# Loading the identity once per head for the scores, and moving a layer's last wo rows in sixteen transfers of eight rows

## The chip, the cores and the metric

The kernel runs on one core of one Trainium2 chip. The metric is the device time of one execution in microseconds (us), lower is better. A profiled run gives a trace; the *span* that its page states is about 2 us shorter than the measured time of the same run. Runs of a one-core program are called fast or slow by how they stand to the fastest run of the same kernel.

## The reference

Four attention layers for one token, in the order A, B, A, B. Each has 32 heads, a cache of 8,192 positions and a head width of 192; the model width is 640. Everything is bfloat16.

```python
def layer(x, k_cache, v_cache, wq, wo):              # cut: names, the key and value repeat (factor 1)
    q = (layernorm(x) @ wq).reshape(B, Sq, 32, 192).transpose(0, 2, 1, 3)
    scores = einsum("bhqd,bhkd->bhqk", q, k_cache) * 192 ** -0.5
    o = einsum("bhqk,bhkd->bhqd", softmax(scores), v_cache)
    return o.transpose(0, 2, 1, 3).reshape(B, Sq, 32 * 192) @ wo
x = x + layer(x, *A); x = x + layer(x, *B); x = x + layer(x, *A); x = x + layer(x, *B)
```

K and V of one head are 3 MB each, and nearly all of them are read in every layer that uses them. So the kernel reads 849 MB and does little arithmetic on each byte.

## The kernel before

All large transfers are issued by one sequencer, SP, into eight buffers `slot[0..7]` of 128 partitions x 24,576 bytes. A K or V tile fills one buffer, one packet of 24,576 bytes for each partition (32,000 such packets in the trace, for 250 tiles). In the trace each transfer adds 16 increments to its semaphore (4,544 for 284 transfers), within 8.6 us for one V tile at the turn of layers; I take each for the landing of the share of one of the 16 DMA engines that the page counts. A reader waits for all 16. SP issues a transfer as soon as the buffer's last reader is done.

The wo matrix of a layer comes in three transfers of 10 heads each and a small last one, "wol", with the rows of the last two heads. It goes into unused columns of the third one's buffer:

```python
if n[0] == "wol":
    wol = slot[place[("wo", l, 2)]][:, NW * D:(NW + OI) * D].rearrange("p (i n) -> p i n", n=D)
    return SP.op(lambda s: s.dma_start(
        wol, w["wo"][o["wol"] * DH:(o["wol"] + O_LAST) * DH].rearrange("(p i) n -> p i n", p=P)),
        sem=semOL, inc=16)
```

OI is 3, so this is 128 partitions x 3 x 640 elements of 2 bytes, 3,840 bytes for each partition.

The scores of a head: DVE multiplies K by q in four chunks; PE then adds up the products over the head width, with the identity as stationary matrix, in 24 matmuls of 512 columns:

```python
for c in range(4):
    PE.wait(chunks[c])
    for r in range(QD // R):
        d0 = c * QD + r * R
        fin = c == 3 and r == QD // R - 1
        e = PE.op(lambda t, d0=d0, fin=fin: t.matmul(S[:, :], lhsT=ident[:], rhs=k3[:, :, d0:d0 + R],
                                                     start=(d0 == 0), stop=fin), signal=fin, bank=use[f"S{par}"])
```

Each of these matmuls is two instructions: a weight load (PEld) of `ident` and the matmul proper (3,072 of each on the page below).

## Time and profile before

| what | value |
|---|---|
| time | 2005.2 us, median of 3 runs (2005.04 to 2006.86) |
| bytes read | 849.35 MB, 424 GB/s over the span |
| main DMA queue (q1) | busy 99.2% of 16 engines' span |
| PE program refills (q8) | 82 packets, 1.34 MB |
| PE busy, DVE busy | 70%, 52% |

These are lines of the page of the kernel before. The first line of part 1 gives busy time, share of the span and number of instructions of each engine; GB/s is by 40 equal slices of the span; then come two DMA queues (packets, MB, share of 16 engines) and two groups of instructions (busy us, mean ns of one, idle time before them).

```profile
PE 1402.4 (70%) x10438; PEld 616.8 (31%) x10438; DVE 1047.3 (52%) x1072; ACT 217.2 (11%) x657; POOL 4.6 (0%) x22
...
GB/s 404 431 430 430 429 430 426 430 431 429 425 431 429 431 429 430 426 431 430 429 361 431 430 430 430 431 426 429 429 430 426 430 428 428 431 430 431 430 430 325
...
q1 hardware_dynamic: 43824, 849.37, 99.2%
q8 instruction: 82, 1.34, 0.3%
...
L437 PE MATMUL S<-slot,ident 128*128 128x512 bf16 x3072 | 839.5, 429 | 286.6 <-DVE slot L425 286.6
L437 PEld LDWEIGHTS S<-slot,ident 128*128 128x128 bf16 x3072 | 307.8, 108 | 813.2 <-DVE slot L425 428.3
```

What to see: the DMA engines have no spare time, at 430 GB/s in nearly every slice. Only the first slice, the one at the turn from layer 1 to layer 2 (361) and the last fall clearly short. The 3,072 weight loads overlap PE's matmuls. So only what DMA engines do can change the time much.

SP's timeline at the end of layer 1 (start, us, line; x2 means two issues):

```profile
1004.11 0.33 SPq L269 DMA_DIRECT2D slot<-in_B_wo_dram  x1
1004.48 0.43 SPq L252 DMA_DIRECT2D slot<-in_B_wo_dram  x1
1009.29 15.91 SPq L264 DMA_DIRECT2D slot<-in_A_wq_dram  x2
```

And the end of the chain of waits (start, us, what):

```profile
1996.69 1.44 PE TB L503 x12
1998.13 3.71 PE YB L394 x90
2001.86 0.16 DVE x_bf L548
```

The last work is PE's output projection (YB).

One more reading, of the 16 increments of a semaphore, is not printed by any view, but the trace has it. The 16 shares of the first K tile land within 1.1 us. Those of a V tile issued at 987.51 land over 8.6 us (1006.65 to 1015.26), and those of the last K tile over 8.2 us (1967.86 to 1976.03). Refills do this: each packet of 16,384 bytes takes about 1.0 to 1.1 us on one engine, and that engine then stays about 1.55 us behind.

### The profile page before, as it was taken

How to read it: one execution, taken by the hardware profiler on the slowest of the kernel's cores; microseconds unless marked ns; L12 is line 12 of the kernel's file. 1: busy time of each engine (PE TensorE's matmuls, PEld its weight loads, DVE VectorE, ACT ScalarE, POOL GpSimd, SP SyncE). 2: the span in 40 equal slices, each digit the busy share in tenths (PEclk: the TensorE clock that was granted, in tenths of full speed). 3: DMA queues.
4: the chain of work that ended last, by engine and by line, in shares of the span. 5: the costliest groups of instructions: out<-in, count | busy, mean ns of one | idle time of the engine just before them, and what ended most of it. 6: DMA issues, size and time to landing. Idle time of an engine off the chain costs nothing.

```text
span 2005.0 us, 23356 instructions
## 1 busy us (share of the span) xinstructions
PE 1402.4 (70%) x10438; PEld 616.8 (31%) x10438; DVE 1047.3 (52%) x1072; ACT 217.2 (11%) x657; POOL 4.6 (0%) x22
## 2 busy tenths in 40 slices
PE   5677767767666767667777676676777767767667
PEld 2223223223332322322342232232234323323223
DVE  3454554556345456455536545545654455654554
ACT  0011011011011111111100111111110111111110
POOL 0000000000000000000000000000000000000000
PEclk9788888788678788878778888888886888987887
DMA  9999999999999999999989999999999999999997
GB/s 404 431 430 430 429 430 426 430 431 429 425 431 429 431 429 430 426 431 430 429 361 431 430 430 430 431 426 429 429 430 426 430 428 428 431 430 431 430 430 325
DMA packets 44067, 850.85 MB, mean 424 GB/s; under 512 B 4800, under 2 KB 7360, under 8 KB 7872
## 3 DMA queue, kind: packets, MB, share of 16 engines
q1 hardware_dynamic: 43824, 849.37, 99.2%
q8 instruction: 82, 1.34, 0.3%
q14 instruction: 17, 0.14, 0.0%
q10 hardware_dynamic: 144, 0.00, 0.0%
HBM read 849.35 MB, written 0.00 MB: 424 GB/s over the span
## 4 chain that ended last, share of the span: by engine, by line
DMA 67%; PE 19%; DVE 12%; ACT 1%; issue 1%; another core or an unknown queue 0%; POOL 0%; DVEq 0%; ACTq 0%
DMA slot<-in_A_k_cache_dram 33%; DMA slot<-in_B_k_cache_dram 32%; PE S L437 13%; DVE slot L425 10%; PE O L473 2%; DMA slot<-in_A_wq_dram 1%; PE TB L488 1%; DVE s_sb L444 1%; DMA x_bf<-in_A_x_dram 1%; ACT p_sb L454 1%; PE QT L358 1%; PE YB L394 1%; PE TB L458 0%; DVE small L451 0%
## 5 line engine op out<-in xcount | busy, mean ns | idle before, releaser
L425 DVE TENSOR_TENSOR slot<-slot,q_sb 128x3072 bf16<-128x3072 bf16 x512 | 865.9, 1754 | 461.2 <-DMA slot<-in_A_k_cache_dram 236.2
L437 PE MATMUL S<-slot,ident 128*128 128x512 bf16 x3072 | 839.5, 429 | 286.6 <-DVE slot L425 286.6
L437 PEld LDWEIGHTS S<-slot,ident 128*128 128x128 bf16 x3072 | 307.8, 108 | 813.2 <-DVE slot L425 428.3
L473 PE MATMUL O<-slot,p_sb 128*2 128x384 bf16 x4096 | 347.0, 420 | 0.0
L444 DVE TENSOR_REDUCE s_sb<-S 128x64 f32<-128x512 f32 x128 | 88.4, 691 | 248.6 <-PE S L437 248.6
L473 PEld LDWEIGHTS O<-slot,p_sb 128*2 128x2 bf16 x4096 | 128.5, 88 | 133.4 <-issue 97.6
L488 PE MATMUL TB<-o_sb,small 128*1 128x192 f32 x480 | 121.5, 385 | 36.6 <-DVE small L462 28.2
L384 ACT ACTIVATE q_sb<-QM 128x192 bf16<-128x192 f32 x120 | 39.6, 330 | 982.4 <-PE QM L377 982.4
L458 PE MATMUL TB<-small,ones 128*128 128x1 f32 x256 | 50.1, 265 | 110.0 <-ACT p_sb L454 110.0
L448 PE MATMUL QM<-ident,m_bf 128*128 128x128 bf16 x128 | 27.8, 217 | 129.6 <-DVE m_bf L447 129.6
L481 ACT ACTIVATE o_sb<-O,small 128x384 f32<-128x384 f32 x128 | 74.3, 580 | 231.0 <-PE O L473 231.0
L462 DVE RECIPROCAL small<-TB 128x1 f32<-128x1 f32 x128 | 21.6, 169 | 122.7 <-PE TB L458 122.7
L458 PEld LDWEIGHTS TB<-small,ones 128*128 128x128 f32 x256 | 39.3, 193 | 129.7 <-ACT p_sb L454 129.7
L454 ACT ACTIVATE p_sb<-s_sb,small 128x64 bf16<-128x64 f32 x128 | 44.5, 348 | 290.1 <-DVE small L451 290.1
L451 DVE TENSOR_REDUCE small<-QM 128x1 f32<-128x128 f32 x128 | 37.3, 292 | 53.7 <-PE QM L448 53.7
L494 ACT ACTIVATE orow<-TB 1x192 bf16<-1x192 f32 x120 | 38.3, 319 | 202.6 <-PE TB L488 202.6
L488 PEld LDWEIGHTS TB<-o_sb,small 128*1 128x1 f32 x480 | 33.2, 88 | 78.4 <-DVE small L462 37.4
L448 PEld LDWEIGHTS QM<-ident,m_bf 128*128 128x128 bf16 x128 | 12.3, 96 | 146.5 <-ACT q_sb L384 131.6
L394 PE MATMUL YB<-oT,slot 128*128 128x1 bf16 x900 | 37.9, 178 | 3.4 <-ACT oT L409 2.2
L394 PEld LDWEIGHTS YB<-oT,slot 128*128 128x128 bf16 x900 | 36.9, 131 | 4.2 <-ACT oT L409 2.9
L377 PEld LDWEIGHTS QM<-ident,qT 128*128 128x128 bf16 x240 | 23.0, 99 | 30.5 <-issue 1.9
L377 PE MATMUL QM<-ident,qT 128*128 128x128 bf16 x240 | 30.4, 209 | 1.6 <-ACT qT L366 1.6
(46 smaller groups left out, 191.0 us busy)
## 6 DMA issues: line engine op xcount, KB each, us to landing
slot<-in_B_k_cache_dram SPq DMA_DIRECT2D x64, 3072.0 KB, 36.1
slot<-in_A_k_cache_dram SPq DMA_DIRECT2D x63, 3072.0 KB, 23.4
slot<-in_A_v_cache_dram SPq DMA_DIRECT2D x63, 3072.0 KB, 25.9
slot<-in_B_v_cache_dram SPq DMA_DIRECT2D x60, 3072.0 KB, 37.5
slot<-in_A_wo_dram SPq DMA_DIRECT2D x6, 2400.0 KB, 26.7
slot<-in_B_wo_dram SPq DMA_DIRECT2D x6, 2400.0 KB, 34.9
slot<-in_A_wq_dram SPq DMA_DIRECT2D x4, 2880.0 KB, 22.5
slot<-in_B_wq_dram SPq DMA_DIRECT2D x4, 2880.0 KB, 29.7
```

What stands on the lines that cost most here:

```text
L377: e = PE.op(lambda t, b=b, o=o, n=n, d=done: t.matmul(QM[:, d:d + n], lhsT=qT[:, b:b + 1].broadcast_to([P, P]), rhs=ident[:, o:o + n], sta ...
L384: lambda a: a.activation(q_sb[i][:], QM[:, 0:DH], ACT.Copy), e, last["q"][i], bank=use["QM"])
L394: e = PE.op(lambda t, i=i, c=c, f=y_first[0], fin=fin: t.matmul(YB[:, c:c + 1], lhsT=t3[:, i, c:D:DC], rhs=o[:, i:i + 1], start=f, stop=fi ...
L425: e = DV.op(lambda v, d0=d0: v.tensor_tensor(k3[:, :, d0:d0 + QD], kin[:, :, d0:d0 + QD], q_sb[qi][:, d0:d0 + QD].unsqueeze(1).broadcast_t ...
L437: e = PE.op(lambda t, d0=d0, fin=fin: t.matmul(S[:, :], lhsT=ident[:], rhs=k3[:, :, d0:d0 + R], start=(d0 == 0), stop=fin), signal=fin, ba ...
L444: ev_s = DV.op(lambda v: v.tensor_reduce(s_sb[par][:], S[:].rearrange("p (j r) -> p j r", r=R), AX.X, ALU.add), ev_S[h], last["s"][par], b ...
L448: e = PE.op(lambda t: t.matmul(QM[:, C_MX:C_MX + P], lhsT=m_bf[par][:, 0:1].broadcast_to([P, P]), rhs=ident[:], start=True, stop=True), ev ...
L454: ev_p[h] = AC.op(lambda a: a.activation(p_sb[par][:], s_sb[par][:], ACT.Exp, bias=negm[par][:, 0:1], accum_out=l_col[par][:]), ev_n, ev_s ...
L458: e = PE.op(lambda t: t.matmul(TB[:, C_L + par:C_L + par + 1], lhsT=ones[:], rhs=l_col[par][:], start=True, stop=True), ev_p[h], last["L"] ...
L473: e = PE.op(lambda e, g=g, j=j, f=m < G, fin=fin: e.matmul(OB[par][32 * g:32 * g + 2, 0:2 * DH], lhsT=p_sb[par][:, j:j + 2], rhs=t[:, j * ...
L481: lambda a: a.activation(o_sb[:], OB[par][:, 0:2 * DH], ACT.Copy, scale=rl[par][:, 0:1]),
L488: e = PE.op(lambda t, i=i: t.matmul(TB[0:1, C_O:C_O + DH], lhsT=pick[:, i:i + 1], rhs=o_sb[:, i * DH:(i + 1) * DH], start=(i == 0), stop=( ...
```

## The change

The intent is, first, to load the identity once per head and let 23 of 24 score matmuls use what the PE array already holds. Second, wol's one transfer becomes 16 transfers of 8 rows each. Each is meant to be served by only 8 engines, so that the idle front-runners may take load from the others.

```diff
+def matmul_held(t, out, lhsT, rhs, start, stop):
+    return t.add_instruction(mybir.InstMatmult(
+        ...                      # cut: name, engine, operands, tile size and position
+        start_tensor_calc=start, stop_tensor_calc=stop, ldweights=False))
@@ wol
-                return SP.op(lambda s: s.dma_start(
-                    wol, w["wo"][o["wol"] * DH:(o["wol"] + O_LAST) * DH].rearrange("(p i) n -> p i n", p=P)),
-                    sem=semOL, inc=16)
+                src = w["wo"][o["wol"] * DH:(o["wol"] + O_LAST) * DH].rearrange("(p i) n -> p i n", p=P)
+                for r in (r + b for r in range(0, P, 32) for b in range(4)):
+                    e = SP.op(lambda s, r=r: s.dma_start(wol[r:r + 29:4], src[r:r + 29:4]), sem=semOL, inc=16)
+                return e
@@ scores
-                        e = PE.op(lambda t, d0=d0, fin=fin: t.matmul(S[:, :], lhsT=ident[:], rhs=k3[:, :, d0:d0 + R],
-                                                                     start=(d0 == 0), stop=fin), signal=fin, bank=use[f"S{par}"])
+                        e = PE.op(lambda t, d0=d0, fin=fin: (
+                            t.matmul(S[:, :], lhsT=ident[:], rhs=k3[:, :, d0:d0 + R], start=True, stop=fin) if d0 == 0 else
+                            matmul_held(t, S[:, :], ident[:], k3[:, :, d0:d0 + R], False, fin)), signal=fin, bank=use[f"S{par}"])
```

More of the change, by code (lines that the diff above doesn't have):

```diff
@@ L53, in emit @@
                     ins.then_inc(it[1], it[2])
+def matmul_held(t, out, lhsT, rhs, start, stop):
+    return t.add_instruction(mybir.InstMatmult(
+        name=t.bass.get_next_instruction_name(), engine=mybir.EngineType.PE,
+        ins=[t.lower_ap(rhs), t.lower_ap(lhsT, for_matmul_weights=True)], outs=[t.lower_ap(out)],
+        start_tensor_calc=start, stop_tensor_calc=stop, tile_size=(128, 128), tile_position=(0, 0), ldweights=False))
 HEADS_W = 10
```

## The prediction

> **What bounds the kernel now.** Transfers: the page shows 849 MB on the main queue, 99.2% of 16 engines' time, 430 GB/s in nearly every slice; only the first slice, the one at the turn from layer 1 to 2 (361) and the last (325) fall clearly short. In the chain of waits DMA has 67%, and DVE waits 2 to 3 us for each K tile. So what counts is when the *last* of the 16 engines delivers its share. The trace's semaphore landings show how unequal they are: the 16 increments of the first K tile arrive within 1.1 us, those of the last V tiles of layer 1 within 8.6 us (1006.7 to 1015.3), within 1.6 us after the turn of layers, within 8.2 us at the end (K head 31: 1967.9 to 1976.0). About eight engines lag 6 to 8.6 us, about six not at all.
>
> The lag comes from the second queue, "instruction": 82 packets of 16,384 bytes, 1.0 to 1.1 us each, about every 24 us. 82 x 16,384 bytes over PE's 20,876 instructions is 64 bytes each, so this is PE's program being refilled[...]. Where one falls, one engine's landing moves back by 1.54 to 1.56 us for good, until queues run dry at the turn.
>
> **What the change does.**
> 1. Held identity: 128 heads x 23 = 2,944 weight loads fewer. On PE they are hidden: six warm 512-column matmuls take 1.47 us, about 216 ns apart, and in a cold stretch about 427 ns apart, weight loads beside them. PE gains next to nothing. But 2,944 x 64 bytes is 11.5 refills less: 11.5 x 1.55 us over about eight lagging engines is 2.2 us (estimate).
> 2. The wo rows: 16 issues of about 0.33 us instead of one of 0.43 us, 4.9 us more on a sequencer that mostly waits for buffers. At the turn 1 to 2 they start at 1004.5 and the next issue is at 1009.3, so at most about 0.5 us slips. Eight rows should give a transfer eight engines[...]. A row of 3,840 bytes takes 149 ns, so eight engines lose 8 x 0.149 = 1.2 us a layer and eight gain as much. [...]
>
> **Critical path.** What lagging engines save reaches the end: the last K tile lands earlier and the 29 us after it stay. Gain 2.2 us plus 0 to 3.6 us; I put 3 in 4 on the favourable engines. So near 2001 us, 0.2% faster.
>
> **What would show it.** Refills near 70; weight loads 7,494; matmul spacing unchanged; spread of landings about 5 us at the turn and 6 to 7 us at the end instead of 8.6 and 8.2; wo rows of layer 3 landed before the previous transfer's slowest share.
>
> **What would make it wrong.** Eight rows served by lagging engines (then about 2006 us); small transfers that cost far more than their bytes; a lower PE clock with fewer PE instructions, which lengthens the tail by 1 to 2 us; a queue sequencer held up at the turn of layers.

The forecast's sum was 2.2 us from the refills plus 0 to 3.6 us from the rows (three layers of 1.2 us), and with 3 in 4 on the second term near 2001 us. The second term needs the engines that serve eight rows to be those that lead. That was the assumption, which no trace of the kernel before shows. Eight engines for eight rows was an assumption as well.

## More of the kernel before

The next view counts busy time in stretches around the end of layer 0, where the wo rows of that layer land. After the stretch and its length come busy us and instructions of PE, PEld, DVE, ACT, POOL; then the granted PE clock, the DMA engines' busy share and GB/s.

```profile
490.00:505.00 15.00, 12.00 (x55) 5.34 (x57) 11.28 (x14) 0.88 (x4) 0.00 (x0) 0.93 1.01 430
505.00:520.00 15.00, 12.49 (x184) 8.94 (x177) 1.36 (x11) 1.50 (x4) 0.55 (x1) 0.53 1.01 428
520.00:535.00 15.00, 10.28 (x62) 3.87 (x59) 8.14 (x8) 1.17 (x4) 0.00 (x0) 0.73 1.01 426
```

The one 128-row transfer of the wo rows (507 to 514 us) leaves no dent: 428 GB/s.

## The result, and the profile after

| | median us | range | runs |
|---|---|---|---|
| before, same rounds | 2006.03 | 2005.04 to 2007.02 | 4 |
| after | 2014.1 | 2011.47 to 2014.65 | 4 |

The ratio is 1.0038, with a 95% interval of 1.002 to 1.0055. Ratios here and below are the mean time of one kernel's fast runs over that of the other's of the same rounds, so they are not quite the ratio of the medians that are quoted. The kernel is 0.4% slower, where 0.2% faster was predicted.

The same parts of the page of the kernel after:

```profile
PE 1404.1 (70%) x10438; PEld 321.1 (16%) x7494; DVE 1047.2 (52%) x1072; ACT 217.6 (11%) x657; POOL 4.7 (0%) x22
...
GB/s 404 431 431 429 431 430 425 429 431 431 397 431 430 430 429 430 426 431 430 430 338 429 429 430 429 432 428 429 429 430 398 431 428 431 430 428 430 430 431 331
...
q8 instruction: 70, 1.15, 0.2%
...
L58 PE MATMUL S<-slot,ident 128*128 128x512 bf16 x2944 | 802.6, 427 | 33.7 <-DVE slot L434 33.6
...
L447 PEld LDWEIGHTS S<-slot,ident 128*128 128x128 bf16 x128 | 12.7, 99 | 337.0 <-DVE slot L434 329.7
```

The weight loads fell to 7,494 and the refills to 70, as meant, and a matmul takes what it took. The loss stands in the GB/s row: three slices fell, slice 11 (425 to 397), slice 21 (361 to 338) and slice 31 (426 to 398). These are the ends of layers 0, 1 and 2. The others are within 3 of what they were, but for the last (325 to 331).

The stretches at the end of layer 0, after:

```profile
490.00:505.00 15.00, 11.79 (x79) 1.54 (x39) 9.76 (x13) 1.00 (x5) 0.00 (x0) 0.96 1.00 430
505.00:520.00 15.00, 9.91 (x149) 7.85 (x150) 0.95 (x9) 1.38 (x4) 0.00 (x0) 0.50 1.02 339
520.00:535.00 15.00, 9.97 (x29) 0.63 (x6) 7.93 (x8) 0.73 (x2) 0.55 (x1) 0.61 0.99 420
```

In the stretch with the wo rows the engines are busy all the time (share 1.02), but they move 339 GB/s instead of 428. That is 15 x (428 - 339) / 428 = 3.1 us of transfers lost. They did not wait; packets took longer, as their records below show.

SP's timeline at the end of layer 1, and the end of the chain, both after:

```profile
1006.15 0.33 SPq L278 DMA_DIRECT2D slot<-in_B_wo_dram  x1
1006.52 10.65 SPq L262 DMA_DIRECT2D slot<-in_B_wo_dram  x16
1017.22 12.36 SPq L273 DMA_DIRECT2D slot<-in_A_wq_dram  x2
```

```profile
1972.12 36.39 DMA slot<-in_B_wo_dram
2008.51 0.14 issue
2008.64 0.75 PE YB L403 x15
2009.41 0.16 DVE x_bf L558
```

The 16 issues take 10.65 us (623 ns for one), where I had put 4.9 us, and the next issue starts 7.9 us later than before. At the end, the last 15 matmuls wait for the last wo rows, which landed at 2008.51. Both look like suspects. Experiments show that the first is none.

The packet records of the trace say which packets got longer. Around the landing of wol in layer 0:

| packets of | before, mean ns | after, mean ns | extra engine time, us (over 149, 717 and 914 ns) |
|---|---|---|---|
| 3,840 B (the wo rows) | 151 | 224 | 9.6 |
| 19,200 B (the wo transfer ahead) | 718 | 893 | 11.3 |
| 24,576 B (K and V around it) | 933 | 1,505 | 29.5 |

Together that is 50.4 us of engine time, or 3.2 us for each of 16 engines in the mean. The same sum is 37.9 us at the end of layer 1 (there mostly packets of wq, 11,520 bytes) and 52.6 us at that of layer 2, so 2.4 and 3.3 us. The three make 8.8 us. The landings of the first tile behind wol agree: the mean of its 16 increments is later than before by 2.83 us after layer 0, 5.48 us after layer 1, 8.56 us after layer 2 (the last increment by 2.45, 5.69 and 8.46 us); the program ends 7.6 us later in these traces. So longer packets account for the loss, and the rows themselves make up less than a fifth of what they cost in layer 0.

### The profile page after: what moved, and what is told of

Its sections match the earlier page's. It is cut to its first block, busy times and chain, and to the rows that moved or that the text cites. A ratio compares the mean times of both kernels' runs of the same rounds, so it can differ in the third digit from the quotient of the medians.

```text
span 2012.6 us, 20472 instructions
## 1 busy us (share of the span) xinstructions
PE 1404.1 (70%) x10438; PEld 321.1 (16%) x7494; DVE 1047.2 (52%) x1072; ACT 217.6 (11%) x657; POOL 4.7 (0%) x22
## 4 chain that ended last, share of the span: by engine, by line
DMA 68%; PE 17%; DVE 12%; SPq 2%; ACT 1%; issue 1%; another core or an unknown queue 1%; POOL 0%; DVEq 0%; ACTq 0%
DMA slot<-in_A_k_cache_dram 33%; DMA slot<-in_B_k_cache_dram 31%; PE S L58 12%; DVE slot L434 10%; DMA slot<-in_B_wo_dram 2%; SPq L262 2%; PE O L483 2%; DMA slot<-in_A_wq_dram 1%; PE S L447 1%; PE TB L498 1%; DVE s_sb L454 1%; DMA x_bf<-in_A_x_dram 1%; ACT p_sb L464 0%; PE TB L468 0%
## 5 line engine op out<-in xcount | busy, mean ns | idle before, releaser
L58 PE MATMUL S<-slot,ident 128*128 128x512 bf16 x2944 | 802.6, 427 | 33.7 <-DVE slot L434 33.6
L447 PE MATMUL S<-slot,ident 128*128 128x512 bf16 x128 | 60.0, 469 | 251.8 <-DVE slot L434 251.7
L447 PEld LDWEIGHTS S<-slot,ident 128*128 128x128 bf16 x128 | 12.7, 99 | 337.0 <-DVE slot L434 329.7
L403 PE MATMUL YB<-oT,slot 128*128 128x1 bf16 x900 | 37.9, 178 | 7.5 <-DMA slot<-in_A_wo_dram 4.5
```

Source lines behind the costliest of these rows:

```text
L58: return t.add_instruction(mybir.InstMatmult(name=t.bass.get_next_instruction_name(), engine=mybir.EngineType.PE, ins=[t.lower_ap(rhs), t. ...
L403: e = PE.op(lambda t, i=i, c=c, f=y_first[0], fin=fin: t.matmul(YB[:, c:c + 1], lhsT=t3[:, i, c:D:DC], rhs=o[:, i:i + 1], start=f, stop=fi ...
L447: t.matmul(S[:, :], lhsT=ident[:], rhs=k3[:, :, d0:d0 + R], start=True, stop=fin) if d0 == 0 else
```

## The experiments

Fourteen runs. All are edits of the kernel before, and "loss" is the median minus that of the kernel before on the same chip. What the traces say of engines is the count of increments. The 64 transfers of wol in the kernel after gave 576, nine each. In layer 0, 16 of them come one with each issue (478.90 to 489.42 us) and 128 with the rows (507.97 to 517.27 us), so eight with the rows of each transfer, and I take these eight for eight engines. Which engine writes which partition is in no trace. The author assumed an order.

### Which half of the change

Theory: the split transfers lose more than held weights gain. Rival: fewer weight loads change the clock or PE's order, and that costs.

`held_only` is the change to the scores alone; `split_only` is the change to wol alone.

```diff
# held_only: the scores of the change, wol as before
# split_only: wol of the change, the scores as before
+for r in (r + b for r in range(0, P, 32) for b in range(4)):
+    e = SP.op(lambda s, r=r: s.dma_start(wol[r:r + 29:4], src[r:r + 29:4]), sem=semOL, inc=16)
```

> The kernel before with the identity held and the wo rows still in one transfer. My prediction's step 1: 70 refills of PE's program instead of 82, 2.2 us less, so about 2 us faster than before (ratio 0.998 to 0.9995). Rival: PE's clock or the weights held in the array change something else, and part of the 8 us loss comes from here: then 1.001 or more.

> The kernel before with the 16 transfers of 8 rows alone, every identity load kept. Theory: the whole loss is here, about 8 + 2 = 10 us slower than before (ratio 1.004 to 1.006). Rival (held identity has a share in the loss): 8 us or less slower, with the identity alone not faster.

Measured: `held_only` 2003.13 us against 2005.8 (ratio 0.9987, 0.997 to 1.0004); `split_only` 2016.26 us (1.0052, 1.0037 to 1.0067). So the split loses 10.5 us. The held identity gained 2.7 by the medians, but its interval reaches over 1. The sum of the two fits the 8 us of the whole change. The clock, the rival, did not move: 0.826 to 0.830 were granted in the four runs of `held_only`, 0.823 to 0.834 in those before. The refills of `held_only` from its page:

```profile
q8 instruction: 70, 1.15, 0.2%
```

The gain was too small for three rounds, so I ran the same kernel again in five, as `held_again`, and the reverse: 46 short weight loads added to each head, `more_loads`.

```diff
+                for _ in range(46):
+                    PE.op(lambda t: t.ldweights(ident[:, 0:32]), signal=False)
```

> The held identity alone once more, with five rounds, because three left its gain of 2.7 us unresolved. Refill theory: 1.5 to 3 us faster than before (ratio 0.9985 to 0.9993), better than both kernels. Rival: no difference outside the interval.

> The kernel before with 46 idle weight loads of 32 columns more per head, 5,888 in all: 23 more refills of PE's program (105 instead of 82) with hardly any array time. Refill theory (each refill costs one engine 1.55 us and the same eight or so engines take them): spread of landings up by a quarter to a third, 3 to 5 us slower. Rival (refills hide; the held identity won by something else): within 1 us of before.

Measured: `held_again` 2005.16 against 2005.62 us (0.9997, 0.9985 to 1.001). `more_loads` 2012.01 us (1.0031, 1.0017 to 1.0044), a loss of 6.4 us where I had expected 3 to 5. Its page shows the refills:

```profile
q8 instruction: 105, 1.72, 0.3%
```

So 23 refills more cost 6.4 us, about 0.28 us each, but 12 fewer gained only 0.5 to 2.7 us, not resolved from nothing. The landings show the lag itself: in `more_loads` the spread grew from 8.6 to 11.0 us at the turn and from 8.2 to 10.7 us at the end, the quarter to a third that was expected. With fewer refills the middle of the lagging engines came closer: 7.7 to 8.3 us behind the first engine at the turn became 6.4 to 6.8 in `held_only` and 6.5 to 7.2 in `held_again`. The slowest engine, for which readers wait, gained less: 8.6 became 8.4 and 8.2 there, and 8.2 became 8.5 and 7.8 at the end. That may be why so little was gained, but two traces do not settle it. `more_loads` also has 46 instructions more on PE in each head (5,888 in all, 92 ns each), and I did not separate these from the refills.

### Is it the number of engines, the number of issues, or the bytes of a piece?

`split16` takes 8 transfers of 16 rows, 8 partitions apart, meant to give all 16 engines equal work (an estimate from the next test, `tags`, where k rows gave k increments and one more, for k up to 15). `rows_half` takes two transfers of 64 rows. `cols_three` takes three transfers of all 128 partitions with pieces of 1,280 bytes. The texts speak of a port theory, later called the owner theory: the guess that the cost arises where a row is written by another engine than in a transfer over all 128 partitions. No run shows a port or an owner; the runs vary only the partitions that the rows go to.

```diff
# split16
+for r in range(8):
+    e = SP.op(lambda s, r=r: s.dma_start(wol[r:r + 121:8], src[r:r + 121:8]), sem=semOL, inc=16)
# rows_half
+for r in (0, 64):
+    e = SP.op(lambda s, r=r: s.dma_start(wol[r:r + 64], src[r:r + 64]), sem=semOL, inc=16)
# cols_three
+for i in range(OI):
+    e = SP.op(lambda s, i=i: s.dma_start(wol[:, i, :], src[:, i, :]), sem=semOL, inc=16)
```

> The kernel before with the wo rows in 8 transfers of 16 rows that are 8 partitions apart[...]. Theory A (the loss comes from eight engines carrying all of it, some of them laggards[...]): most of the loss is gone, under 2 us slower than before; an issue costs about 0.33 us, a row 149 ns. Theory B (small transfers cost far more than their bytes): 3 us or more slower, with rows still taking 149 ns but spaced apart.

> The kernel before with the wo rows in two transfers of 64 whole rows (partitions 0 to 63, then 64 to 127). [...] Port theory[...]:[...] rows and neighbours near double time, 1 to 2 us lost in each of layers 0 to 2, 3 to 6 us slower (ratio 1.0015 to 1.003). Rival (many small transfers and their increments are what costs): two transfers cost what one does, within 1 us of before.

> The kernel before with the wo rows in three transfers, each of all 128 partitions and a third of every row (1,280 bytes). Three times as many pieces and two issues more[...]. Port theory: rows and neighbours keep their time, within 1 us of before. Rival (splitting costs in itself): 2 us or more slower.

| kernel | median us | ratio (95%) | loss us | GB/s, 505 to 520 us |
|---|---|---|---|---|
| `split16` | 2015.86 | 1.0049 (1.0034 to 1.0064) | 10.1 | 345 |
| `rows_half` | 2016.92 | 1.0054 (1.0039 to 1.0069) | 11.1 | 322 |
| `cols_three` | 2006.78 | 1.0005 (0.999 to 1.002) | 0.9 | 423 |

`split16`, meant to load all engines equally, loses as much: uneven load does not look like the cause, and `low_half` below (eight rows a transfer, a loss of 2.1 us) says so with less assumed. (Neither of its theories came true as written: the loss is not under 2 us, and its rows took 224 ns in layer 0, not 149.) `rows_half` has only two issues: neither is the number of issues. (It lost 11.1 us where the port theory asked for 3 to 6.) `cols_three` has pieces a third as long, three times as many, and loses nothing that can be resolved: neither is the size of a piece. What `cols_three` shares with the kernel before is that each transfer covers all 128 partitions. So the next theory is that it matters which partitions a transfer covers. That is what the port theory comes to, as far as runs can show it.

`rows_half` lost its 11 us over four layers on 0.5 MB each, and in the stretch that its trace shows the engines did not wait; the packets were longer: 322 GB/s at a busy share of 1.02.

### Are the front-runners among engines 0 to 7?

`tags` sends tiny transfers with 1, 2, ... 15 rows at three places. The numbers of engines here are only names: engine k is the one whose increment is new with k + 1 rows. That a transfer of one more row keeps the engines of the one before, and that the eight of a wol transfer are engines 0 to 7 in this sense, is assumed and shown by no run.

```diff
+                for k in range(15):
+                    e = SP.op(lambda s, k=k, c0=c0: s.dma_start(tags[0:k + 1, c0:c0 + 32], w["wo"][0:k + 1, 0:32]), sem=semT[k], inc=16)
```

> The kernel before with, at three points, 15 tiny transfers of 1, 2, ... 15 rows. [...] My prediction assumed that engines 0 to 7 lead and 8 to 15 lag. Theory now: laggards are spread over both halves, so 0 to 7 hold both leaders and engines 6 us or more behind. Rival: 0 to 7 are the laggards as a block.

Measured (one run, state unknown, 2007.02 us against 2005.8): transfers of k rows gave k + 1 increments, which I take for k engines and the one that comes with the issue. At head 24 of layer 1 the tags landed, in us, in this order of engines (about 0.19 us are taken off for each tag up to its own, since they land one behind the other):

```text
8: 896.3   7: 896.9   2: 898.5   4: 898.8   0: 899.3   1: 900.9   3: 901.7
9 to 12: 901 to 902   14: 902.7   13: 902.8   6: 903.6   5: 905.6
```

In layer 3 engines 5 and 6 lag again, and 8, 7, 0, 2 and 4 lead. So engines 0 to 7 hold four leaders and also the two worst laggards of the 15 engines that the tags reach. If the assumption holds, my 3 in 4 for "the eight that serve the rows lead" was wrong, and a load of 1.2 us more on all eight would fall on engines 5 and 6 as well.

### Where the rows go

The author expected, by the assumed order of engines, that the split's rows 0 to 63 are free and its rows 64 to 127 pay. Three kernels with the same 16 issues and the same bytes send the rows elsewhere. `low_half` sends all to partitions 0 to 63, `high_half` all to 64 to 127, `low_shift` those of `low_half` four partitions higher. Half of the rows go to a spare tile (another tile gave up 8 of its 48 columns to make room). **All three compute with wrong wo rows on purpose**; the comparison's tolerance let them pass all the same, so their "correct" means nothing.

```diff
# low_half ("0 <= r" and "r < 64"; high_half has 64 and 128)
+    to, at = (wol, r) if 0 <= r < 64 else (spare3, (r + 64) % P)
+    e = SP.op(lambda s, r=r, to=to, at=at: s.dma_start(to[at:at + 29:4], src[r:r + 29:4]), sem=semOL, inc=16)
# low_shift
+    to, at = (wol, r + 4) if r < 64 else (spare3, r - 60)
```

> Wrong result on purpose: the 16 transfers of 8 rows with every row written to partitions 0 to 63 (half of them into a spare tile). [...] Port theory: rows take 149 ns, no neighbour is slowed; what is left is 1.2 us more for laggards 5 and 6 per layer and the issue time at the turn, 2 to 6 us slower than before, clearly less than the split alone (10.5). Rival (the eight engines' own load or the small pieces are what costs): as slow as the split alone.

> Wrong result on purpose: the same with every row written to partitions 64 to 127[...]. Port theory:[...] rows near 300 ns, neighbours near double; slower than the split alone by 3 us or more (13 us or more over before). Rival: the same as with the low half.

> Wrong result on purpose: the low half run with every transfer moved up by 4 partitions (4 to 35 and 36 to 67)[...]. Owner theory[...]: rows near 300 ns and neighbours slowed, 15 us or more over before, as in the high half run. Half theory (only partitions 64 to 127 are slow for engines 0 to 7): rows near 149 ns, 2 to 4 us over before, as in the low half run.

| kernel | median us | ratio (95%) | loss us | a wo row, layer 0, mean ns |
|---|---|---|---|---|
| `low_half` | 2007.96 | 1.0011 (0.9994 to 1.0028) | 2.1 | 149 |
| `split_only` | 2016.26 | 1.0052 (1.0037 to 1.0067) | 10.5 | 226 |
| `low_shift` | 2023.35 | 1.0088 (1.0071 to 1.0104) | 17.0 | 244 |
| `high_half` | 2027.14 | 1.0108 (1.0093 to 1.0123) | 21.3 | 281 |

The stretch of 505 to 520 us in `low_half`, then in `high_half`, then in `low_shift`:

```profile
505.00:520.00 15.00, 12.48 (x181) 8.73 (x174) 1.14 (x11) 1.50 (x4) 0.00 (x0) 0.50 1.01 425
```

```profile
505.00:520.00 15.00, 11.05 (x157) 7.28 (x158) 0.17 (x1) 1.50 (x4) 0.00 (x0) 0.61 1.02 277
```

```profile
505.00:520.00 15.00, 11.59 (x174) 7.96 (x167) 0.02 (x1) 1.51 (x4) 0.00 (x0) 0.50 1.02 338
```

The same sixteen transfers run at 425, 277 or 338 GB/s, by nothing but the partitions they go to. With rows to partitions 0 to 63 only, each of the 512 rows took less than 165 ns; with rows to 64 to 127 only, the loss is 21.3 us, twice that of the split (10.5), which has half of its rows there. The step of four partitions from `low_half` to `low_shift` keeps 60 of the 64 partitions within the lower half, and the loss grows from 2.1 to 17.0 us. So a rule by halves is refuted: a step of four partitions was enough. That fits the guess about engines, but does not show it. (In GB/s `low_shift` loses 3.2 us in this stretch, but that is the mean of the engines; the slowest one landed 4.8 us later than before behind it.)

`low_half` also clears SP. Its timeline at the end of layer 1 has the same slow issues:

```profile
1003.17 5.33 SPq L257 DMA_DIRECT2D slot<-in_B_wo_dram  x8
1008.54 5.29 SPq L257 DMA_DIRECT2D spare<-in_B_wo_dram  x8
1013.87 20.27 SPq L268 DMA_DIRECT2D slot<-in_A_wq_dram  x3
```

The wq issue comes 4.6 us later than before, and the first K tile after the turn of layers lands no later (0.15 us earlier). So the 10.7 us of issues aren't on the critical path.

### Two tests that did not come out as expected

`eight_next` takes 16 transfers of 8 neighbouring rows.

```diff
+for r in range(0, P, 8):
+    e = SP.op(lambda s, r=r: s.dma_start(wol[r:r + 8], src[r:r + 8]), sem=semOL, inc=16)
```

> The kernel before with the wo rows in 16 transfers of 8 neighbouring rows (0 to 7, 8 to 15, ...)[...]. Port theory[...]:[...] rows over 300 ns, 20 us or more slower than before. Rival (partitions 64 to 127 are slow for the low engines[...]): half of the rows are slow, as in the split with a step of 4, about 10.5 us slower. The step also tells why an issue took 0.62 us: if the step of 4 is the reason it falls to about 0.3.

Measured: 2017.28 us against 2005.62 (1.0058, 1.0042 to 1.0073), a loss of 11.7 us, where the owner theory asked for 20 or more and the rival for 10.5. A row took 210 ns in layer 0, and 356 GB/s were moved from 505 to 520 us. So the owner theory, as counted, does not give the size of the loss. Patterns that cover all 128 partitions in steps of 1, 4 and 8 lost 11.7, 10.5 and 10.1 us, while the three with all rows in 64 partitions (`low_half`, `low_shift`, `high_half`) lost 2.1, 17.0 and 21.3. I did not test why. One by-product: these issues took 0.295 us each against 0.623, so it is the step of the partitions, not the number of rows, that made an issue slow here.

`late_rows` was to test SP's time at the turn: it moves the 16 issues of layer 1 behind the first wq transfer of layer 2.

```diff
-                plan += [("wq", l, g) for g in range(len(Q_PARTS))]
+                plan += [("wq", l, 0), ("wol", l - 1)] + [("wq", l, g) for g in range(1, len(Q_PARTS))]
-            plan.append(("wol", l))
+            if l != 1:
+                plan.append(("wol", l))
```

> The split of 8 rows, a step of 4 apart, with layer 1's 16 issues moved behind the first wq transfer of layer 2, which waited 10.7 us behind them. If the queue's sequencer is on the critical path at the turn of layers, 2 to 3 us are won back (7.5 to 8.5 over before). Port theory alone: no change beyond 1 us (10 to 11 over before), because the low half run lost nothing at the turn with the same issues.

Measured: 2020.0 us (1.0071, 1.0057 to 1.0085), 14.4 us lost. The test was badly designed: the first wq was issued at 1013.52 and landed until 1032.8, the rows came behind it, the projection waited for them, and the next wq could be issued only at 1037.06. It says nothing for or against SP. `low_half` answered that question.

### One engine that walks over all partitions

`walk` adds three transfers of 127 rows of 3,840 bytes to a spare tile, in the expectation that one engine writes them all, in order of partitions. (The first reading below shows a busy share of 0.08 while the rows run alone, about one engine of 16; the order of partitions is assumed.) By the owner theory the other engines should be slowed one after the other.

```diff
+WALKS = [(0, 12), (0, 26), (2, 12)]
+                walk_ev.append(SP.op(lambda s: s.dma_start(
+                    spare[0:127], w["wo"][0:OI * 127].rearrange("(p i) n -> p (i n)", p=127)), *walk_ev[-1:], sem=semW, inc=16))
```

> The kernel before with three extra transfers of 127 rows of 3,840 bytes into a spare tile, at heads 12 and 26 of layer 0 and 12 of layer 2. [...] Owner theory:[...] at each time one other engine's packets slowed. Half theory: 149 ns up to partition 63, slow from 64 on.

Measured (one run, state unknown): 2070.61 us against 2006.37, about 21 us for each walk. The first walk in stretches:

```profile
195.00:209.50 14.50, 9.23 (x84) 4.08 (x85) 8.31 (x9) 1.56 (x7) 0.00 (x0) 1.00 1.00 427
...
211.50:216.00 4.50, 2.12 (x7) 0.81 (x8) 3.94 (x3) 0.00 (x0) 0.00 (x0) 0.85 0.08 29
216.00:219.00 3.00, 3.00 (x10) 1.13 (x9) 2.83 (x2) 0.00 (x0) 0.00 (x0) 0.66 1.12 356
219.00:230.00 11.00, 3.42 (x18) 1.53 (x16) 1.38 (x4) 1.09 (x4) 0.00 (x0) 0.77 1.00 343
```

SP's timeline beside it:

```profile
177.87 0.33 SPq L256 DMA_DIRECT2D spare<-in_A_wo_dram  x1
183.90 31.64 SPq L270 DMA_DIRECT2D slot<-in_A_v_cache_dram  x1
215.59 1.16 SPq L270 DMA_DIRECT2D slot<-in_A_k_cache_dram  x1
```

The rows start at 209.54 us. Up to about 216 us about one engine works and the others have nothing to do (share 0.08): the V issue behind the walk stays on SP for 31.64 us and ends at 215.54. Then all run together. This gives a comparison within one transfer. In all three walks:

- While the others are idle (share 0.08), the rows take 149 to 162 ns, whichever row it is.
- Once the others run again, rows take about 330, 350, 210 and 195 ns by their place in a group of four, to the end. It begins at the 50th row in the first walk, and fully at the 57th in the other two; the first packets of the others had begun 1 to 2 us earlier.
- In the second walk, where the others had already ended their packets when it began, no one of the first 48 rows is slow. In the first and third, the eighth to tenth row are (172 to 316 ns), at a time when some seven to ten packets were still under way. But the fifth to seventh rows of the first walk took 149 to 162 ns beside eleven or twelve.

So these rows are not slow in themselves (149 to 162 ns alone); they were slow (about 195 to 350 ns) only when other engines were at work, and not in every case then. The last point of the owner theory fails: in the first walk 238 of 269 packets of 24,576 bytes took over 1,050 ns, 1,101 ns in the mean, against 915. (These are the ones begun after the first packet of each engine behind the idle time. Those first ones took 1,402 to 2,126 ns, but so did 15 of the program's first 16 in the kernel before, 1,366 to 2,458 ns.) While this one transfer ran, nearly all large packets were longer, not those of one engine at a time. It fits this that the neighbours lose about four times what the rows lose (40.8 against 9.6 us in layer 0 of the kernel after).

What slows them no run shows: 343 instead of 427 GB/s were moved, and why rows of one place in four take 350 ns and those of another 195 stays open.

## Why the prediction was wrong, point by point

- **The bound: right.** DMA engines are full, and the last of 16 landings counts. The losses of the split came through this.
- **82 refills to 70, weight loads 7,494, matmuls unchanged: right.** Six score matmuls took 1.46 us against 1.47. **The gain of 2.2 us: not shown.** It measured 2.7 us in one set of rounds and 0.5 in the other, neither clear of zero. The estimate shared the refills out over eight engines, but what counts is the slowest one, and in the two traces that one gained little on the first (0.2 and 0.4 us at the turn).
- **"16 issues of about 0.33 us" and "at most about 0.5 us slips": wrong.** They took 0.623 us each and the next issue slipped by several us, because a step of four partitions made an issue slower (0.295 us with neighbouring rows). `low_half` shows that this costs nothing.
- **Eight rows get eight engines: right**, by nine increments for each transfer, eight of them with the rows. Which eight, no run shows. **"3 in 4 on the favourable engines": wrong**, if they are those that `tags` reached with up to eight rows: these hold leaders and the two worst laggards. With rows to partitions 0 to 63 only (`low_half`) the tiles behind wol landed up to 1.0 us later in the trace, which is what engines 5 and 6 would make of 1.2 us more.
- **"A row of 3,840 bytes takes 149 ns, so eight engines lose 8 x 0.149 = 1.2 us a layer and eight gain as much": this is the step that failed.** I read 149 ns from the rows of a transfer over all 128 partitions, and took it for the price of a row in any transfer. In the split a row took 224 ns in the mean in layer 0, and the K and V packets around them went from 933 to 1,505 ns, a cost to neighbours for which the sum has no term. Instead of moving 1.2 us from some engines to others, the rows took 3.2 us from each of the 16 (in the mean) in layer 0, 2.4 at the end of layer 1 and 3.3 in layer 2. The prediction's list of dangers has "small transfers that cost far more than their bytes"; I gave it no number and too little weight.
- **Spread of landings "about 5 us at the turn and 6 to 7 us at the end": wrong.** It was 8.9 us for the V tile at the turn and 8.6 us for the last K tile.
- **"wo rows of layer 3 landed before the previous transfer's slowest share": wrong.** The transfer ahead had landed at 2005.14 us and the rows at 2008.51, and the projection waited for them. The end of the program was late by no more than the last K tile (7.6 against 8.2 us), so this wait is no loss of its own here.

What is settled: the split loses about 10 us because packets get longer while its rows land (`split_only` moved 337 GB/s where the kernel before moved 428, at a busy share of 1.02), and the loss depends on the partitions that the rows go to (2.1 us for 0 to 63, 17.0 four higher, 21.3 for 64 to 127). What is open: whether the held identity gains anything, whether the cause is which engine writes which partition, as guessed, and why the price per row differs between patterns. No version that was run is clearly faster than the kernel before; `held_only` is the only candidate, and its interval reaches over 1.

## What to carry to other kernels

Where DMA engines are full as here (busy 99.2%), try first to keep a transfer over all 128 partitions and, if it must be cut, to cut it by columns: here three column pieces cost nothing that could be measured (0.9 us, interval 0.999 to 1.002), while two row pieces cost 11.1 us and sixteen 10.5 us. Look at GB/s beside the busy share of the DMA engines: a share of 1.0 with fewer GB/s meant here that packets had become longer, not that engines waited, and the packet lengths of the *neighbours* show the true cost. A duration read from a trace holds for the transfer, the place and the traffic in which it was read (a row took 149 ns in one pattern and 281 in another); before you price a new pattern with it, ask which of these the change alters.
